# Float32 quarter products for the last 64 queries, one transpose group for the odd blocks, and new planner numbers, in an attention and gated FFN kernel

## The chip, the cores and the metric

The kernel runs on one core of a Trainium2 chip. The metric is the device time of one execution in microseconds. The engines are TensorE (PE in the profile; PEld is its weight load), VectorE (DVE), ScalarE (ACT), GpSimd (POOL) and SyncE (SP), which issues nearly all DMAs. They run side by side and wait for each other through semaphores; each one works in the order in which its instructions were written.

## The reference, cut to what matters

There are 8 batches of 8 heads with 576 queries and 64 columns a head. Attention keeps only scores within `tau` of the row's maximum; the result goes through a gated FFN with a convolution of three taps over the sequence.

```python
scores = scale * np.matmul(q, k.transpose(0, 1, 3, 2))
thresh = np.max(scores, axis=-1, keepdims=True) - tau
scores = np.where(scores >= thresh, scores, -1000000000.0)
scores = scores - np.max(scores, axis=-1, keepdims=True)
attn = np.exp(scores)
attn = attn / (np.sum(attn, axis=-1, keepdims=True) + 1e-09)
x = np.matmul(attn, v)          # then heads side by side: [8, 576, 512]
h = np.maximum(x @ w_in, 0.0)   # w_in [512, 1024]
for k in range(3):
    conv_out += conv_w[k][None, None, :] * hp[:, k:k + S, :]
gate = 1.0 / (1.0 + np.exp(-conv_out))
return (h * gate @ w_out).astype(np.float32)
```

The FFN's weights and the convolution's come as float64.

## The kernel before, in words

**Tiling.** A batch's 576 queries are cut into five tiles, four of 128 and one of 64, and these into two chunks: tiles 0 and 1 (256 queries), tiles 2, 3 and 4 (320). The eight heads go in four pairs. So a batch has 2 chunks x 4 pairs = 8 pair steps, with 2 or 3 units each, 20 units in a batch. A unit is one query tile of one pair of heads. In a full unit each head has its own PSUM tile; in the unit of 64 queries the two heads share one, 64 partitions each.

**A unit** (`unit`, L408 to L490). PE makes the scores into `ps_s` (two tiles). DVE takes the row maximum (`top`, L448), ACT the exponential into `em` (L454), DVE masks it against the limit and sums (`mask`, L457), POOL normalises it (`norm`, L487). `em` is 128 x 1152: two heads of 576 keys, or nine blocks of 128 columns. There are three `em` tiles in rotation.

**The scores' number formats.** In batch 0 (`plain`) they are float32 products with a contraction of 64, and two halves of the keys stand on the two halves of the partitions (L429): for 128 queries two such products lie in the array together, for 64 queries four, in its quarters. From batch 1 on the inputs are split: `prep_k` (L369) scales k by 1/8 on ACT, rounds it to fp32r and has POOL subtract the rest, into `ks`; `prep_q` (L383) rounds q into `q1` and POOL subtracts the rest into `q2`. The scores are then products with a contraction of 128 (L440), one with `q1` and one with `q2` for each head and half of the keys: four for a head, eight for a unit. In the unit of 64 queries the second head is computed with 128 columns of weights and the first then overwrites the upper partitions; its keys are taken turned by 64, for which `ks` holds 64 columns more.

**Turning and attending.** `transposes` (L492) turns `em` on PE (L509) into `ps_t` (two tiles), four blocks a group, and ACT copies each group to `eT` (L503). A full unit has groups of 4, 4 and 1 blocks; the unit of 64 queries has one of 4 and one of two halves (L533). After a pair's last unit, `attend` (L546) multiplies `eT` with v into `pa` (L555, 20 products), and ACT and DVE write x as a rounded part and a rest.

**FFN.** `mm1` (L572) has 12 products for each of 8 blocks of columns into `ph` (L585), then relu, taps, tanh and gate on ACT, POOL and DVE, and the split into the rings `gh` and `gl`. `mm2` (L641) has 24 products into `po` (L650) for each 128 tokens. The FFN work of a chunk is spread over the units of the next chunk.

**Weights.** `split` (L278) turns sixteen float64 pieces of 512 columns into a rounded part and a rest during the first batch: ACT takes the absolute value, POOL limits it from both sides (`f1`, L302), DVE puts the bits together in three steps (L305, L308, L311), ACT rounds (L319) and POOL subtracts (L263). `WRATE` sets how many pieces a unit of the loop gets, for the first and the second matrix.

**Order.** Nothing is issued in the order of the code. Each operation goes to a planner (`Plan`, L53) with an estimated time, the tiles that it reads and writes, and a rank: the number of its unit, less an `AHEAD` value for its sort of work. The planner simulates the five engines and writes the instructions in the order in which it picked them: on each engine the lowest rank that is ready and has its tile free. On PE it may take an operation up to `KEEP` ranks later that needs no costly change of form (`SWITCH`). DVE may take work meant for POOL when more than `BACKLOG` ns of it wait there. The order on each engine is then fixed, and the hardware follows it whatever the real times are.

Of the kernel before, what the change touches and what calls it, by code (L numbers as in the profile page):

```python
# [19 lines left out]
AHEAD = {'s': 4.5, 't': 4.0, 'a': 3.5, 'prep': 5.5, 'w': 2.0, 'load': 4.0}  # L20
# [4 lines left out]
BACKLOG = {'pool': 10000.0, 'dve': 500.0, 'act': 9e9}  # L25
WRATE = (0.9, 0.65)
ALT = 3.0

# [8 lines left out]
KEEP = 0.6  # L37


class Buf:  # L40
# [6 lines left out]
    def __getitem__(self, key):  # L47
        if self.tile is None:
            self.tile = self.pool.tile(self.shape, self.dtype, tag=self.tag, bufs=self.bufs, name=self.name)
        return self.tile[key]  # L50

# [146 lines left out]
def tile_tau_attention_gated_ffn(  # L198
# [26 lines left out]
    GROUPS = [(0, 1), (2, 3, 4)]  # L225
    CHUNKS = [(0, 255), (255, 321)]
    COLS = [(0, 256), (254, 322)]
    NEW = [(0, 256), (256, 320)]
# [49 lines left out]
    def split(src, n, name, high, low, hr, lr, queue="sp"):  # L278
# [3 lines left out]
        stage = plan.buf(wk, "ks", 4, [P, KW], U32, name)  # L282
        value = plan.buf(wk, "q2", 2, [P, 2, QW], U32, f"{name}_f")

        def words(dtype=U32):
            pairs = stage[:, :2 * n].rearrange("p (f two) -> p f two", two=2)
            return pairs[:, :, 0].bitcast(dtype), pairs[:, :, 1].bitcast(dtype)
# [7 lines left out]
        def load():  # L295
            (nc.sync if queue == "sp" else nc.scalar).dma_start(stage[:, :2 * n].bitcast(I64), src)
# [4 lines left out]
        def f1(e):  # L301
            engines[e].tensor_scalar(v(), v(), TINY, HUGE, op0=ALU.max, op1=ALU.min)  # L302
# [23 lines left out]
    KW, QW = 2 * S + D, max(w for _, w in NEW)  # L326
# [30 lines left out]

    def plain(b):
        return b == 0

    def prep_k0(p, g):

        ks = plan.buf(wk, "xk", 2, [P, S + D], F32, f"ks_0_{p}_{g}")
        a = AHEAD["prep"]
        op("sp", 450, lambda: nc.sync.dma_start(ks[:], kp[p]), w=[(ks, 0)], ahead=a + 2)
        op("act", act(S + D), lambda: nc.scalar.activation(ks[:], ks[:], AF.Copy, scale=0.125), w=[(ks, 0)], ahead=a)
        return ks

    def prep_k(b, p, j, ks):  # L369

        w = S + j * D
        a = AHEAD["prep"]
        xk = plan.buf(wk, "xk", 2, [P, S + D], F32, f"xk_{b}_{p}_{j}")
        part = slice(j * S, j * S + w)
        op("sp", 820, lambda: nc.sync.dma_start(xk[:, :w], kd[b, p, :, j, :w]), w=[(xk, 0)], ahead=a + 2)
        op("act", act(w), lambda: nc.scalar.activation(xk[:, :w], xk[:, :w], AF.Copy, scale=0.125), w=[(xk, 0)], ahead=a)
        op("act", act(w), lambda: nc.scalar.activation(ks[:, part], xk[:, :w], AF.Copy), w=[(ks, j)], r=[(xk, 0)], ahead=a)
        op(
            "pool", pool(w), lambda e: subtract(e, ks[D:, part], xk[D:, :w], ks[D:, part].bitcast(F32)),
            w=[(ks, j)], r=[(xk, 0)], ahead=a, other=[("dve", dve(w))]  # L380
        )

    def prep_q(b, p, j, g, q2):  # L383

        o, w = NEW[g]
        n = f"{b}_{p}_{j}_{g}"
        src = qd[b, p, :, j, o:o + w]
        a = AHEAD["prep"]
        if plain(b):
            q1 = plan.buf(wk, "q1", 4, [P, w], F32, f"q1_{n}")  # L390
            op("sp", 455, lambda: nc.sync.dma_start(q1[:], src), w=[(q1, 0)], ahead=a + 2)
            return q1
        xq = plan.buf(wk, "xq", 2, [P, w], F32, f"xq_{n}")
        q1 = plan.buf(wk, "q1", 4, [P, w], F32R, f"q1_{n}")
        op("sp", 455, lambda: nc.sync.dma_start(xq[:], src), w=[(xq, 0)], ahead=a + 2)
        op("act", act(w), lambda: nc.scalar.activation(q1[:], xq[:], AF.Copy), w=[(q1, 0)], r=[(xq, 0)], ahead=a)  # L396
        op(
            "pool", pool(w), lambda e: subtract(e, q2[:, j, :w], xq[:], q1[:].bitcast(F32)),
            w=[(q2, j)], r=[(xq, 0), (q1, 0)], ahead=a, other=[("dve", dve(w))]
        )  # L400
        return q1

    def load_v(b, p, g):
        vt = plan.buf(wk, "v", 2, [P, NBLK + 1, D], F32, f"v_{b}_{p}_{g}")
        op("sp", 820, lambda: nc.sync.dma_start(vt[:], vc[b, p]), w=[(vt, 0)], ahead=AHEAD["prep"])
        return vt

    def unit(u, k, q1, q2, o, n):  # L408
# [5 lines left out]
        em = plan.buf(wk, "em", 3, [P, 2 * S], F32, f"em_{u}")  # L414
# [4 lines left out]
        for h, js in enumerate(heads):  # L419
# [3 lines left out]
            def mm(js=js, ps=ps):  # L423
                if q2 is None:
                    for r, j in enumerate(js):
                        for c in range(2):
# [3 lines left out]
                                ps[r * n:(r + 1) * n, c, :CH], lhsT=q1[j][on, o:o + n], rhs=k[on, at:at + CH],  # L430
# [3 lines left out]


                for r, j in reversed(list(enumerate(js))):
                    for c in range(2):
                        at = j * S + r * D + c * CH
                        for i, q in enumerate((q1[j][:, o - r * n:o + n], q2[:, j, o - r * n:o + n])):
                            nc.tensor.matmul(  # L440
                                ps[:(r + 1) * n, c, :CH], lhsT=q, rhs=k[:, at:at + CH], start=(i == 0), stop=(i == 1)
                            )
# [13 lines left out]
            def mask(ps=ps, th=th, view=view, total=total):  # L456
# [6 lines left out]
                "pe", 480 if q2 is None else 532 * len(js), mm, w=[(ps, 0)],  # L463
                r=[(x, j if x is not k or q2 is not None else 0) for j in js for x in (k, q2) if x is not None] + [(q1[j], 0) for j in js],
                ahead=a, kind="rows" if q2 is None else "full"
# [26 lines left out]
    def transposes(u, em, n, eT, off):  # L492
        def group(i, js, parts, *evacs):
# [4 lines left out]
                "pe", max(width, 140) * 0.86, lambda: parts(pt), w=[(pt, 0)], r=[(em, j) for j in js] + [(ident, 0)], ahead=AHEAD["t"],  # L498
                kind="turn"
# [7 lines left out]
        def turn(pt, b0, nb):  # L507
            for i in range(nb):
                nc.tensor.transpose(  # L509
                    out=pt[:, i * P:(i + 1) * P], in_=em[:, (b0 + i) * P:(b0 + i + 1) * P], identity=ident[:]  # L510
                )

        if n == P:
            for b0 in range(0, NBLK, 4):
                nb = min(4, NBLK - b0)
                js = [j for j in range(2) if b0 * P < (j + 1) * S and (b0 + nb) * P > j * S]
                group(
                    b0, js, lambda pt, b0=b0, nb=nb: turn(pt, b0, nb),
                    (nb * P, lambda b0=b0, nb=nb: eT[:, b0:b0 + nb, off:off + P],
                     lambda pt, nb=nb: pt[:, :nb * P].rearrange("p (a b) -> p a b", a=nb))  # L520
                )
            return
# [8 lines left out]
        def halves(pt):  # L531
            for j in range(2):
                nc.tensor.matmul(  # L533
                    pt[j * D:(j + 1) * D, :n], lhsT=em[:, 4 * P:4 * P + D], rhs=ident[:, j * n:(j + 1) * n], start=True, stop=True
                )

        group(
            0, [0], lambda pt: turn(pt, 0, 4),
            (4 * P, both, lambda pt: pt[:].rearrange("p (i j n) -> p j i n", i=4, j=2))
        )  # L540
        group(
            1, [0], halves,
            (n, lambda: eT[:, 4, off:off + n], lambda pt: pt[:, :n])
        )
# [27 lines left out]
    def mm1(b, g, f, xs):  # L572
        gh, gl = ring
        k0, kn = CHUNKS[g]
        a0, an = COLS[g]
        fs = slice(f * P, (f + 1) * P)
        n = f"{b}_{g}_{f}"
# [4 lines left out]
        for cb in range(NCB):  # L582
# [8 lines left out]
            op("pe", an * 3 / 2.4 + 40, mm, w=[(ph, 0)], r=ws + [(xs[cb], i) for i in (0, 1, 2) if i < 2 or g], kind="full")  # L591
# [70 lines left out]
    def ffn(c):  # L662

        first = []
        if c < len(chunks):
            b, g = chunks[c]
            first = [(COLS[g][1] * 5, lambda f=f: mm1(b, g, f, xs[c])) for f in range(NFB)]
        ends = [0, EARLY] + [(b * S + sum(CHUNKS[g])) // P for b, g in chunks]
        second = [(5120, lambda m=m: mm2(m)) for m in range(ends[c], ends[c + 1])]
        seq = []  # L670
        n1, n2 = MOE
        if not c:
# [6 lines left out]
    CW = COLS[1][1]  # L679
    xs = {}  # L680
    chunks = [(b, g) for b in range(B) for g in range(2)]
    pairs = [(c, p) for c in range(len(chunks)) for p in range(NP)]
    units = [(i, t) for i in range(len(pairs)) for t in GROUPS[pairs[i][0] % 2]]
    kss, qss, q2s, vts = {}, {}, {}, {}

    def prep(i, j):
# [15 lines left out]
        if j == 0:
            vts[i] = load_v(b, p, g)
# [98 lines left out]
```

## Time and profile before

| | |
|---|---|
| median of 3 runs | 1002.08 us (999.22 to 1002.26) |
| profiled execution | 1003.37 us, span 1001.6 us, mean granted clock 0.977 |
| PE busy | 947.2 us (95%) |
| DVE busy | 802.7 us (80%) |
| POOL busy | 757.7 us (76%) |
| ACT busy | 705.0 us (70%) |
| DMA | 79.00 MB, mean 79 GB/s |

A group's row gives line, engine, operation, what is written and read, shapes and count; then busy time and mean ns of one; then the idle time of the engine before them and who ended it. Matmuls overlap, so that the mean of one is longer than its share. In a timeline a row starts with its start and its duration. A row of a stretch gives, after its bounds and length, the busy time and count of PE, PEld, DVE, ACT and POOL, then the granted clock, the DMA share and GB/s.

### The profile page before, as it was taken

How to read it: one execution, taken by the hardware profiler on the slowest of the kernel's cores; microseconds unless marked ns; L12 is line 12 of the kernel's file. 1: busy time of each engine (PE TensorE's matmuls, PEld its weight loads, DVE VectorE, ACT ScalarE, POOL GpSimd, SP SyncE). 2: the span in 40 equal slices, each digit the busy share in tenths (PEclk: the TensorE clock that was granted, in tenths of full speed). 3: DMA queues.
4: the chain of work that ended last, by engine and by line, in shares of the span. 5: the costliest groups of instructions: out<-in, count | busy, mean ns of one | idle time of the engine just before them, and what ended most of it. 6: DMA issues, size and time to landing. Idle time of an engine off the chain costs nothing.

```text
span 1001.6 us, 19333 instructions
## 1 busy us (share of the span) xinstructions
PE 947.2 (95%) x6368; PEld 766.5 (77%) x6368; DVE 802.7 (80%) x1942; ACT 705.0 (70%) x1544; POOL 757.7 (76%) x1159
## 2 busy tenths in 40 slices
PE   5788868999999999999999999999999999999998
PEld 2445636877888788877888788878888878888796
DVE  4879969998777967998888978898788888898443
ACT  4666668787776776778767777778776777776443
POOL 3878998887877887798677877788767877787343
PEclk9889969999999999999999999999999999999999
DMA  6543224133222232223321233213321231211000
GB/s 197 156 124 122 81 72 124 53 87 98 75 79 60 83 93 65 64 68 90 97 64 58 78 92 91 65 41 106 99 67 58 66 106 46 64 54 38 22 22 32
DMA packets 44739, 79.00 MB, mean 79 GB/s; under 512 B 5216, under 2 KB 21600, under 8 KB 44640
## 3 DMA queue, kind: packets, MB, share of 16 engines
q1 hardware_dynamic: 44208, 76.20, 25.0%
q10 hardware_dynamic: 432, 1.57, 0.5%
q8 instruction: 51, 0.84, 0.3%
q14 instruction: 48, 0.39, 0.1%
HBM read 68.31 MB, written 9.44 MB: 78 GB/s over the span
## 4 chain that ended last, share of the span: by engine, by line
PE 69%; POOL 14%; DVE 9%; issue 4%; ACT 4%; DMA 1%; SPq 0%; POOLq 0%; ACTq 0%
PE po L650 16%; PE ph L585 15%; PE pa L555 13%; PE ps_s L440 12%; PE ps_t L509 12%; POOL em L487 5%; DVE em L457 2%; POOL gl L263 2%; POOL ks L263 2%; DVE few L448 2%; POOL stage_f L302 1%; DVE t L612 1%; POOL q L263 1%; ACT eT L503 1%; PE ps_s L429 1%
## 5 line engine op out<-in xcount | busy, mean ns | idle before, releaser
L487 POOL TENSOR_SCALAR em<-em,few 128x576 f32<-128x576 f32 x288 | 260.5, 912 | 40.3 <-DVE few L482 29.0
L448 DVE TENSOR_REDUCE few<-ps_s 128x1 f32<-128x576 f32 x288 | 212.9, 750 | 66.9 <-PE ps_s L440 51.4
L457 DVE SCALAR_TENSOR_TENSOR em<-ps_s,few,em 128x576 f32<-128x576 f32 x288 | 232.0, 811 | 33.6 <-ACT em L454 28.0
L585 PE MATMUL ph<-x,w1h 128*128 128x322 f32 (+1 forms) x1024 | 254.1, 310 | 1.0 <-DVE x L566 0.8
L503 ACT ACTIVATE eT<-ps_t 128x512 f32<-128x512 f32 (+1 forms) x448 | 200.4, 480 | 63.9 <-PE ps_t L509 60.6
L454 ACT ACTIVATE em<-ps_s,few 128x576 f32<-128x576 f32 x288 | 211.8, 743 | 44.0 <-DVE few L448 33.4
L509 PE MATMUL ps_t<-ident,em 128*128 128x128 f32 x1280 | 206.0, 283 | 20.2 <-POOL em L487 14.6
L509 PEld LDWEIGHTS ps_t<-ident,em 128*128 128x128 f32 x1280 | 154.1, 144 | 63.4 <-POOL em L487 32.9
L440 PE MATMUL ps_s<-ks,q 128*128 128x288 f32 (+1 forms) x1120 | 193.8, 305 | 6.7 <-DVE em L457 6.6
L612 DVE SCALAR_TENSOR_TENSOR t<-hp,cw,t 128x255 f32<-128x255 f32 (+1 forms) x256 | 171.1, 675 | 23.0 <-POOL t L603 19.6
L585 PEld LDWEIGHTS ph<-x,w1h 128*128 128x128 f32 x1024 | 178.8, 190 | 8.2 <-issue 3.6
L555 PE MATMUL pa<-eT,v 128*64 128x256 f32 (+1 forms) x1280 | 174.8, 421 | 1.7 <-ACT eT L503 1.7
L440 PEld LDWEIGHTS ps_s<-ks,q 128*128 128x128 f32 (+1 forms) x1120 | 159.7, 184 | 20.9 <-issue 10.1
L585 PE MATMUL ph<-x,w1l 128*128 128x322 f32 (+1 forms) x512 | 152.1, 297 | 0.0
L555 PEld LDWEIGHTS pa<-eT,v 128*64 128x64 f32 x1280 | 88.2, 140 | 70.2 <-issue 10.2
L263 POOL TENSOR_TENSOR gl<-t,gh 128x321 fp32r<-128x321 f32 (+13 forms) x184 | 118.9, 658 | 23.5 <-ACT gh L629 22.3
L650 PE MATMUL po<-w2h,gh 128*128 128x512 f32 x288 | 121.1, 421 | 0.8 <-ACT w2h L319 0.8
L650 PE MATMUL po<-w2l,gh 128*128 128x512 f32 x288 | 113.9, 396 | 2.0 <-POOL w2l L263 2.0
L650 PE MATMUL po<-w2h,gl 128*128 128x512 f32 x288 | 113.9, 396 | 1.2 <-POOL gl L263 0.8
L263 POOL TENSOR_TENSOR q<-xq,q 128x256 fp32r<-128x256 f32 (+1 forms) x112 | 94.0, 846 | 14.6 <-ACT q L396 8.3
L603 POOL TENSOR_SCALAR t<-hp,cw 128x321 f32<-128x321 f32 (+1 forms) x128 | 72.3, 566 | 43.1 <-ACT hp L600 37.5
L585 PEld LDWEIGHTS ph<-x,w1l 128*128 128x128 f32 x512 | 97.6, 191 | 0.5
(56 smaller groups left out, 1122.8 us busy)
## 6 DMA issues: line engine op xcount, KB each, us to landing
v<-in_vc_dram SPq DMA_DIRECT2D x64, 320.0 KB, 2.9
out_dram<-ot SPq DMA_DIRECT2D x36, 256.0 KB, 2.1
xk<-in_kd_dram SPq DMA_DIRECT2D x28, 320.0 KB, 2.9
xq<-in_qd_dram SPq DMA_DIRECT2D x56, 160.0 KB, 2.2
xk<-in_kd_dram SPq DMA_DIRECT2D x28, 288.0 KB, 2.7
xq<-in_qd_dram SPq DMA_DIRECT2D x56, 128.0 KB, 2.1
stage<-in_w_out_dram SPq DMA_DIRECT2D x8, 512.0 KB, 3.3
ks<-in_kp_dram SPq DMA_DIRECT2D x8, 320.0 KB, 3.8
```

Source lines behind the costliest of these rows:

```text
L263: engines[e].tensor_tensor(dst, x, y, op=ALU.subtract)
L440: nc.tensor.matmul(ps[:(r + 1) * n, c, :CH], lhsT=q, rhs=k[:, at:at + CH], start=(i == 0), stop=(i == 1))
L448: nc.vector.tensor_reduce(few[:rows, nm], ps[:rows, :, :CH], op=ALU.max, axis=mybir.AxisListType.XY, negate=True)
L454: nc.scalar.activation(view(), ps[:rows, :, :CH], AF.Exp, bias=few[:rows, nm])
L457: nc.vector.scalar_tensor_tensor(view(), ps[:rows, :, :CH], few[:rows, th], view(), op0=ALU.is_ge, op1=ALU.mult, accum_out=few[:rows, total])
L487: engines[e].tensor_scalar(sl, sl, few[:rows, 6 + h:7 + h], few[:rows, 8 + h:9 + h], op0=ALU.mult, op1=ALU.add)
L503: "act", act(w, True), lambda dst=dst, src=src: nc.scalar.activation(dst(), src(pt), AF.Copy),
L509: nc.tensor.transpose(out=pt[:, i * P:(i + 1) * P], in_=em[:, (b0 + i) * P:(b0 + i + 1) * P], identity=ident[:])
L555: nc.tensor.matmul(pa[j * D:(j + 1) * D, :w], lhsT=vt[:, blk + j, :], rhs=eT[:, blk, :w], start=(r == 0), stop=(r == 4))
L585: nc.tensor.matmul(ph[:, :an], lhsT=w1[w][:, cb, fs], rhs=xs[cb][:, h, :an], start=(cb == 0 and i == 0), stop=(cb == NCB - 1 and i == 2))
L612: nc.vector.scalar_tensor_tensor(t[:, :kn], hp[:, k:kn + k], cw[:, 3 * f + k:3 * f + k + 1], t[:, :kn], op0=ALU.mult, op1=ALU.add)
L650: nc.tensor.matmul(po[:], lhsT=x[:, f, at:at + P], rhs=w[:, f, :], start=(f == 0 and i == 0), stop=(f == NFB - 1 and i == 2))
```

## The change

- The last unit of a pair (64 queries) has float32 products in quarters of the array in all batches, as in batch 0. For that, `prep_rows` loads k as two halves on the partitions into an `xk` tile and the unit's q into a new tile `q`, and scales q by 1/8 (batch 0 now scales q too, not k). `ks` loses its 64 extra columns, and the split of q covers the 256 queries of full units alone. `q1` is one tile for both heads.
- The ninth block of a pair's full units, and the halves of its unit of 64 queries, are turned in one group after the pair's last unit. `em` has four tiles.
- `f1` takes the smaller of value and upper limit first, and then the larger of that and the lower limit.
- The planner's numbers are others: `AHEAD`, `BACKLOG`, `WRATE`, `KEEP`.
- The chunks are written as a list of named tuples; their cuts and the tokens of each stay the same.

```diff
-AHEAD = {'s': 4.5, 't': 4.0, 'a': 3.5, 'prep': 5.5, 'w': 2.0, 'load': 4.0}
+AHEAD = {'s': 6.0, 't': 3.5, 'a': 3.5, 'prep': 4.0, 'w': 2.0, 'load': 4.25}
-BACKLOG = {'pool': 10000.0, 'dve': 500.0, 'act': 9e9}
-WRATE = (0.9, 0.65)
+BACKLOG = {'pool': 28000.0, 'dve': 500.0, 'act': 9000000000.0}
+WRATE = (0.891, 1.015)
-KEEP = 0.6
+KEEP = 1.2
...
         def f1(e):
-            engines[e].tensor_scalar(v(), v(), TINY, HUGE, op0=ALU.max, op1=ALU.min)
+            engines[e].tensor_scalar(v(), v(), HUGE, TINY, op0=ALU.min, op1=ALU.max)
...
+    def prep_rows(i, b, p, o, w, tag):
+
+        k = plan.buf(wk, "xk", 2, [P, S + D], F32, f"k_{i}")
+        q = plan.buf(wk, tag, 2, [P, 2, w], F32, f"{tag}_{i}")
         a = AHEAD["prep"]
+        op("sp", 450, lambda: nc.sync.dma_start(k[:], kp[b, p]), w=[(k, 0)], ahead=a + 2)
+        op("sp", 450, lambda: nc.sync.dma_start(q[:], qd[b, p, :, :, o:o + w]), w=[(q, 0)], ahead=a + 2)
+        op("act", act(2 * w), lambda: nc.scalar.activation(q[:], q[:], AF.Copy, scale=0.125), w=[(q, 0)], ahead=a)
+        return k, q
...
-        em = plan.buf(wk, "em", 3, [P, 2 * S], F32, f"em_{u}")
+        em = plan.buf(wk, "em", 4, [P, 2 * S], F32, f"em_{u}")
...
                             nc.tensor.matmul(
-                                ps[r * n:(r + 1) * n, c, :CH], lhsT=q1[j][on, o:o + n], rhs=k[on, at:at + CH],
+                                ps[r * n:(r + 1) * n, c, :CH], lhsT=q1[on, j, o:o + n], rhs=k[on, at:at + CH],
                                 start=True, stop=True
                             )
                     return
-
-
-                for r, j in reversed(list(enumerate(js))):
-                    for c in range(2):
-                        at = j * S + r * D + c * CH
-                        for i, q in enumerate((q1[j][:, o - r * n:o + n], q2[:, j, o - r * n:o + n])):
-                            nc.tensor.matmul(
-                                ps[:(r + 1) * n, c, :CH], lhsT=q, rhs=k[:, at:at + CH], start=(i == 0), stop=(i == 1)
-                            )
+                for c in range(2):
+                    for i, q in enumerate((q1, q2)):
+                        nc.tensor.matmul(
+                            ps[:, c, :CH], lhsT=q[:, h, o:o + n], rhs=k[:, h, c * CH:(c + 1) * CH], start=(i == 0), stop=(i == 1)
+                        )
...
+        if len(ems) < tiles:
+            return
+        full = [x for x in ems if x[1] == P]
+        w = len(full) * P
+
+        def odd(pt):
+            for i, x in enumerate(full):
+                turn(pt, i * P, x[0], 8)
+            if n < P:
+                halves(pt, w)
+
+        parts = [(w, lambda: eT[:, 8, :w], lambda pt: pt[:, :w])]
+        if n < P:
+            parts.append((n, lambda: eT[:, 4, off:off + n], lambda pt: pt[:, w:w + n]))
+        group(8, [(x[0], 1) for x in full] + ([(em, 0)] if n < P else []), odd, *parts)
...
+            if not o:
+                prep_k(b, p, j, whole[i][0])
+            prep_q(i, b, p, j, *whole[i][1:])
+            if j and w % P:
+                last[i] = (*prep_rows(i, b, p, o + w - w % P, w % P, "q"), None)
```

More of the change, by code (lines that the diff above doesn't have):

```diff
@@ L1 @@
+import collections
 import heapq
@@ L50, in __getitem__ @@
         return self.tile[key]
+Chunk = collections.namedtuple("Chunk", "b tiles new cols tokens done")
 class Plan:
@@ L222, in tile_tau_attention_gated_ffn @@
     TILES = [(t * P, min(P, S - t * P)) for t in range((S + P - 1) // P)]
[L225 to L228, printed above, removed]
+    chunks = []
+    for b in range(B):
+        for tiles in FIRST if not b else GROUPS:
+            o = TILES[tiles[0]][0]
+            end = sum(TILES[tiles[-1]])
+            a0, k0 = max(o - 2, 0), max(o - 1, 0)
+            chunks.append(Chunk(
+                b=b, tiles=tiles, new=(o, end - o), cols=(a0, end - a0), tokens=(k0, (end if end == S else end - 1) - k0),
+                done=(b * S + (end if end == S else end - 1)) // P
+            ))
+    XW = [max(c.cols[1] for c in chunks[i::2]) for i in range(2)]
+    CW = max(XW)
     cpool = ctx.enter_context(tc.tile_pool(name="cpool", bufs=1))
@@ L325, in tile_tau_attention_gated_ffn @@
     WN = 512
-    KW, QW = 2 * S + D, max(w for _, w in NEW)
+    QW = 2 * P
     n3 = 3 * NFB
@@ L490, in unit, with transposes, group @@
         return em
-    def transposes(u, em, n, eT, off):
-        def group(i, js, parts, *evacs):
+    def transposes(u, ems, tiles, eT):
+        em, n, off = ems[-1]
+        def group(i, reads, parts, *evacs):
             pt = plan.buf(ps_t, "ps_t", 2, [P, 512], F32, f"ps_t_{u}_{i}")
@@ L497, in group @@
             op(
[L498 to L499 removed]
+                "pe", max(width, 140) * 0.86, lambda: parts(pt), w=[(pt, 0)], r=reads + [(ident, 0)], ahead=AHEAD["t"], kind="turn"
             )
@@ L505, in group, with turn, turns @@
                 )
[L507 to L522, printed above, removed]
+        def turn(pt, at, em, b):
+            nc.tensor.transpose(out=pt[:, at:at + P], in_=em[:, b * P:(b + 1) * P], identity=ident[:])
+        def turns(pt, b0):
+            for i in range(4):
+                turn(pt, i * P, em, b0 + i)
         def both():
@@ L665, in ffn @@
         if c < len(chunks):
[L666 to L669, printed above, removed]
+            first = [(chunks[c].cols[1] * 5, lambda f=f: mm1(c, f, xs[c])) for f in range(NFB)]
+        done = [chunks[i].done if i >= 0 else 0 for i in (c - 2 + (c - 1 < EARLY), c - 1 + (c < EARLY))]
+        second = [(5120, lambda m=m: mm2(m)) for m in range(*done)]
         seq = []
         n1, n2 = MOE
-        if not c:
+        if c < EARLY:
             return first + second
@@ L677, in ffn @@
         return seq
-    CW = COLS[1][1]
     xs = {}
-    chunks = [(b, g) for b in range(B) for g in range(2)]
     pairs = [(c, p) for c in range(len(chunks)) for p in range(NP)]
-    units = [(i, t) for i in range(len(pairs)) for t in GROUPS[pairs[i][0] % 2]]
-    kss, qss, q2s, vts = {}, {}, {}, {}
+    units = [(i, t) for i in range(len(pairs)) for t in chunks[pairs[i][0]].tiles]
+    whole, last, vts = {}, {}, {}
     def prep(i, j):
@@ L735, in tile_tau_attention_gated_ffn @@
                 attend(i, eT, vts[i], w, x, off)
-            if t == GROUPS[g][0]:
-                prep(i + 1, 0)
-            if t == GROUPS[g][1]:
-                prep(i + 1, 1)
-            if t == GROUPS[g][-1] and p == NP - 1:
+            for j in range(2):
+                if t == tiles[min(j, len(tiles) - 1)]:
+                    prep(i + 1, j)
+            if t == tiles[-1] and p == NP - 1:
                 seq = ffn(c)
@@ L744, in tile_tau_attention_gated_ffn @@
                 for ns, fn in seq:
-                    work.append((now + 1 + at / total * NP * len(GROUPS[1 - g]), fn))
+                    work.append((now + 1 + at / total * NP * len(chunks[min(c + 1, len(chunks) - 1)].tiles), fn))
                     at += ns
```

140 lines of the change are left out of this document (62 added, 78 removed).

## The prediction

> **What bounds the kernel now.** I read the page's busy shares first, then the busy time by stretch, then the chain of waits of the start.
>
> ```profile
> PE 947.2 (95%) x6368; PEld 766.5 (77%) x6368; DVE 802.7 (80%) x1942; ACT 705.0 (70%) x1544; POOL 757.7 (76%) x1159
> ```
>
> TensorE leads, but a mean over stages hides that there are two regimes:
>
> ```profile
> 0.00:25.00 25.00, 12.54 (x54) 6.90 (x56) 11.98 (x34) 11.67 (x21) 9.18 (x23) 1.00 0.61 197
> 25.00:125.00 100.00, 83.02 (x513) 52.98 (x510) 87.73 (x201) 64.64 (x130) 84.88 (x95) 0.88 0.38 121
> 125.00:175.00 50.00, 37.06 (x202) 26.14 (x201) 39.85 (x86) 35.30 (x71) 43.18 (x45) 0.80 0.33 98
> 200.00:900.00 700.00, 692.56 (x4835) 578.41 (x4834) 584.06 (x1444) 525.65 (x1170) 550.55 (x867) 1.00 0.25 76
> 900.00:1001.60 101.60, 97.38 (x596) 80.74 (x594) 55.19 (x124) 48.15 (x113) 48.85 (x98) 0.99 0.08 28
> ```
>
> The columns are busy PE, weight loads, DVE, ACT and POOL, then the granted clock. From 200 to 900 us PE is busy 692.56 of 700 at clock 1.00, while DVE, ACT and POOL have 16 to 25% of their time free. There the end moves only with PE's own instructions, or with its 7.4 us of idle time. Before 175 us it is otherwise: PE idles 12.5 + 17.0 + 12.9 = 42.4 us, and its clock falls to 0.88 and 0.80, while DVE and POOL are 80 to 88% busy. In that time the sixteen weight pieces are split and PE has little FFN work to fill it.
>
> ```profile
> by line: issue 9.7%; POOL em L487 9.6%; PE pa L555 8.2%; PE ps_t L509 7.0%; POOL stage_f L302 6.7%; DVE em L457 5.6%; PE ps_s L429 4.9%; DVE few L448 4.2%; DMA ks<-in_kp_dram 3.0%; POOL ks L263 2.9%; ACT eT L503 2.8%; DVE stage_f L308 2.6%;
> L302 POOL TENSOR_SCALAR stage_f<-stage_f x16: 1915/1942/2335, 13.0 to 144.3; 128x512 f32<-128x512 f32 x16
> ```
>
> This is the chain of the first 200 us. The two limits of the weights (L302) hold 6.7% of it, 13.4 us; each takes 1.94 us.
>
> **The quarters.** In batches 1 to 7 the unit with the last 64 queries is eight single-pass (fp32r) products of 288 columns. In batch 0 it is already four float32 products in quarters of the array, which the trace records as eight. Both forms can thus be timed, from the first start to the start of the next group:
>
> ```profile
> 311.62 1.22 PE L440 MATMUL ps_s<-ks,q 128*128 128x288 f32 x8
> 312.67 0.31 PE L585 MATMUL ph<-x,w1h 128*128 128x322 f32 x1
> ```
> ```profile
> 88.16 0.28 PE L585 MATMUL ph<-x,w1h 128*128 128x256 f32 x1
> 88.37 0.71 PE L429 MATMUL ps_s<-ks,q 64*64 64x288 f32 x8
> 89.02 0.39 PE L585 MATMUL ph<-x,w1h 128*128 128x256 f32 x1
> 89.24 0.28 PE L585 MATMUL ph<-x,w1l 128*128 128x256 f32 x1
> 89.36 0.28 PE L585 MATMUL ph<-x,w1h 128*128 128x256 f32 x1
> ```
>
> Now: 312.67 − 311.62 = 1.05 us. In quarters: 89.02 − 88.37 = 0.65 us, and the change of form costs on both sides. The `ph` product ahead of it waits 0.21 us for its successor and the one behind it 0.22, where the interval 89.24 to 89.36 is 0.12; so 0.09 + 0.10 are added and a unit costs 0.84. The gain is 0.21 us. There are 28 such units (7 batches, 4 pairs), all in the stretch that PE bounds: **−5.9 us**. Bounds: with the crossings free, 28 × (1.05 − 0.65) = 11.2; with crossings that eat all of it, 0. I take the measured crossing, as the neighbours in batch 1 to 7 are the same `ph` and transposes.
>
> [...]
>
> **The odd blocks in one group.** The ninth 128-column block of each full unit had a transpose, a PSUM tile and an evacuation of its own. Now the odd blocks of a pair's units share one group. On PE that is no gain, since a lone transpose costs hardly more than itself:
>
> ```profile
> 304.57 0.32 PE L585 MATMUL ph<-x,w1h 128*128 128x322 f32 x1
> 304.73 0.27 PE L509 MATMUL ps_t<-ident,em 128*128 128x128 f32 x1
> 304.76 0.39 PE L585 MATMUL ph<-x,w1h 128*128 128x322 f32 x1
> 304.99 0.31 PE L585 MATMUL ph<-x,w1l 128*128 128x322 f32 x1
> 305.14 0.31 PE L585 MATMUL ph<-x,w1h 128*128 128x322 f32 x1
> ```
>
> From 304.57 to 304.99 are 0.42 us with two `ph` products of 0.15 (304.99 to 305.14) in it: 0.12 us for the transpose. In a group of eight each further one takes (1.03 − 0.27)/7 = 0.11:
>
> ```profile
> 302.51 1.03 PE L509 MATMUL ps_t<-ident,em 128*128 128x128 f32 x8
> ```
>
> So joining the odd blocks of 64 pairs saves at most some 64 × 2 × 0.01 = 1.3 us on PE; I take 0. ACT loses two evacuations of 128 columns a pair and gains one of 256:
>
> ```profile
> L503 ACT ACTIVATE eT<-ps_t 128x128 f32<-128x128 f32 x128 | 35.6, 278 | 6.9 <-PE ps_t L509 6.4
> L503 ACT ACTIVATE eT<-ps_t 128x512 f32<-128x512 f32 x288 | 169.7, 598 | 57.0 <-PE ps_t L509 54.2 <-ACT xk L376 0.2
> ```
>
> Between these rows a column costs 0.83 ns, so 256 take about 385 ns: 35.6 − 64 × 0.385 = 11 us less of ACT's 705. ACT is idle a quarter of the long stretch, so this moves nothing; if ACT were the bound it would be worth the 11 us. What the edit may cost is the life of `em` (fourth rival).
>
> **Splitting and loading for the last units.** POOL's second subtraction per pair shrinks from 640 to 576 columns, and the q split of the second chunk from 320 to 256:
>
> ```profile
> L263 POOL TENSOR_TENSOR ks<-xk,ks 64x640 fp32r<-64x640 f32 x28 | 46.2, 1652 | 1.7
> L263 POOL TENSOR_TENSOR ks<-xk,ks 64x576 fp32r<-64x576 f32 x28 | 41.0, 1463 | 2.2
> L263 POOL TENSOR_TENSOR q<-xq,q 128x320 fp32r<-128x320 f32 x56 | 51.3, 923 | 8.6 <-ACT q L396 4.2 <-ACT eT L503 2.2 <-ACT x L563 1.6
> L263 POOL TENSOR_TENSOR q<-xq,q 128x256 fp32r<-128x256 f32 x56 | 42.7, 770 | 6.0 <-ACT q L396 4.1 <-ACT xk L376 1.4 <-ACT eT L503 0.2
> ```
>
> That is 28 × 0.19 + 56 × 0.15 = 14 us less on POOL, off the path after 200 us (POOL 550 of 700 busy) and 1.4 us of it before 175. ACT saves about as many columns on the same edits as its 28 new scalings of 128 columns of q (0.28 us each by the 128-column row) add: nothing. SP issues 28 more loads of k (320 KB) and 28 of q (64 KB). They sit in SP's queue ahead of the next pair's q and v loads, and the k tile holds one of the two `xk` buffers until the quarters have read it. A load of that size takes 2.9 us to land here, and a unit of the loop lasts (938.3 − 148.3)/140 = 5.6 us by the next row (1120 products, eight a unit); that covers it: 0. Without that cover it is 28 × 2.9 = 81 us at the worst, which I do not believe, as the DMA share is 0.25.
>
> ```profile
> L440 PE MATMUL ps_s<-ks,q x1120: 288/295/580, 148.5 to 938.4; 128*128 128x288 f32 x167, 128*64 128x288 f32 x20
> xk<-in_kd_dram SPq DMA_DIRECT2D x28, 320.0 KB, 2.9
> ```
>
> **The order of limits.** The same two immediates on POOL, min first and then max. The trace has no min-first row. Nearest rows: 1.94 us for max-first, and 0.83 us, the median of a multiply-add over 576 columns:
>
> ```profile
> L487 POOL TENSOR_SCALAR em<-em,few x288: 811/829/1810, 15.2 to 943.2; 128x576 f32<-128x576 f32 x144
> ```
> It is thus worth 0 to 16 × 1.1 = 18 us of POOL, all before 146 us. I take 0: same operations, same count. [...]
>
> **Planner numbers.** The pieces of the second weight matrix come at ranks 1/1.015 apart, not 1/0.65: the eighth at 9.0 + 7.9 = 16.9 units, not 21.2. Today the first output product runs while these pieces arrive:
>
> ```profile
> 126.52 0.50 PE L650 MATMUL po<-w2h,gh 128*128 128x512 f32 x1 [0.77 <-ACT w2h L319]
> ...
> 128.62 0.50 PE L650 MATMUL po<-w2l,gh 128*128 128x512 f32 x1 [1.37 <-POOL w2l L263]
> ...
> 137.48 1.12 PE L509 MATMUL ps_t<-ident,em 128*128 128x128 f32 x4 [2.33 <-ACT w2h L319]
> ...
> 140.83 0.80 PE L650 MATMUL po<-w2l,gh 128*128 128x512 f32 x1 [0.67 <-POOL w2l L263]
> 141.56 5.60 PE L555 MATMUL pa<-eT,v 128*64 128x320 f32 x20
> ```
>
> Direct waits on w2: 0.77 + 1.37 + 2.33 + 0.67 = 5.1 us. After them the `pa` group of 20 takes 5.60 us, at the lowered clock; by the next row a group takes 97.5/32 = 3.05 (640 products, 20 each): 2.6 more. Up to 7.7 us can go.
>
> ```profile
> L555 PE MATMUL pa<-eT,v 128*64 128x320 f32 x640 | 97.5, 453 | 1.7 <-ACT eT L503 1.7
> ```
> But the pieces move into 75 to 125 us, where DVE and POOL are 88 and 85% full, and there the limits alone cost POOL 1.94 us a piece and delay a softmax. Lower bound −7.7, upper +5 (two pieces' POOL and DVE time that finds no gap). I take **−4**. The other ranks, the larger backlog before DVE takes POOL's work, and PE's wider choice (KEEP 1.2) only reorder work; in the dense stretch they can win no more than the 7.4 us of idle time and I take 0.
>
> **Sum.** The profiled execution took 1003.37 us, 1.8 beyond its span; −5.9 − 4.0 gives 993.5. The runs' median lies 1.3 below the profiled time: **992.2 us**.
>
> **The rivals.**
> 1. *Min-first is cheap on POOL.* For it: a multiply-add over more columns takes 0.83 us on the same engine. Against: symmetry. It frees 18 us of POOL before 146 us. L302's 13.4 us in the chain is the most that can return; DVE, 88% busy there, keeps some back, so I take 10. Time 982, 974 to 990.
> 2. *Nothing arrives.* PE's 0.21 us a unit turns into idle time because the score tiles wait for DVE's mask, and the earlier w2 gives back at the start what it took. For it: PE's waits for `em L457` exist already. Against: 5.9 us of PE work less, with 116 us of free DVE time in the long stretch. Time 1000.5, 999 to 1004.
> 3. *The softmax tile becomes the bound, slower.* A pair of three units now holds three of four `em` tiles until its last unit is normalised on POOL, because the odd group comes then; only one tile is left for the next pair, where three rotated freely before. Behind the odd group in PE's order stand the pair's `pa` products, which read what it evacuates.
>
> ```profile
> PE ps_t L509 <- POOL em L487: 14.6, 18, 3.7
> ```
>
> Each such wait of PE costs 14.6/18 = 0.8 us today. If 16 of the 32 three-unit pairs add one, that is 13 us, and net of the quarters +7: 1009 us, 1005 to 1020. It decides from eight pairs on (8 × 0.8 > 5.9). Against: PE has FFN work to run instead, and the order is planned with that tile count.
>
> **How the numbers follow.** This kernel's three runs span 0.3%, so 0.3% (3 us) is what a measurement can tell from no change. Chances: forecast 0.44 (992, own range 985 to 1000), rival 1 0.28, rival 2 0.14, rival 3 0.14. Faster than 999.1: 0.40 of the forecast's 0.44, all of rival 1, 0.01 of rival 2: 0.69. Within 0.3%: 0.04 of the forecast and 0.11 of rival 2. Slower: 0.02 of rival 2 and rival 3: 0.16. The range runs from rival 1's lower edge to the near half of rival 3: 974 to 1007.
>
> **What would show it.** Right: the 64-query group from its first start to the next group is 0.65 us in all batches, with 0.2 us intervals on both sides; PE busy in 200 to 900 stays above 98.5%; the last w2 wait of PE ends before 135 us. The new L302 row settles rival 1: under 1.2 us it holds, at 1.9 it is out. Rival 3 shows as PE waits on `em L487` above 30 us in all. The forecast is wrong if the start (PE idle before 175 us, 42.4 now) grows, or if the quarters among fp32r products show more than 0.9 us.

## The result and the profile after

The changed kernel takes **978.31 us** (977.8 to 978.69, 4 runs) against 1001.87 us before (999.22 to 1002.26): a ratio of 0.977, 95% interval 0.9753 to 0.9788. The profiled execution took 977.8 us with a span of 976.0, that is 25.6 us less than before. The forecast was 992 us: right in sign, and less than half of the gain. The result lies below the 985 to 1000 us that the forecast gave itself; it is inside the whole range only because rival 1's 974 to 990 us was added to it.

The busy time of the changed kernel by stretch (columns as before):

```profile
0.00:25.00 25.00, 9.07 (x33) 5.06 (x33) 11.24 (x25) 11.32 (x21) 9.46 (x27) 1.00 0.66 219
25.00:125.00 100.00, 82.27 (x540) 51.46 (x540) 90.44 (x210) 69.00 (x133) 79.81 (x107) 0.93 0.39 123
125.00:175.00 50.00, 43.41 (x293) 34.89 (x293) 46.47 (x111) 39.89 (x82) 45.34 (x57) 0.93 0.32 95
...
200.00:900.00 700.00, 694.16 (x4911) 569.31 (x4911) 598.17 (x1459) 526.15 (x1163) 546.00 (x894) 1.00 0.29 88
900.00:976.00 76.00, 71.91 (x421) 60.04 (x419) 33.56 (x70) 30.71 (x75) 27.73 (x56) 1.00 0.07 25
```

The first 175 us in one row, before and then after:

```profile
0.00:175.00 175.00, 132.63 (x764) 86.02 (x765) 139.56 (x319) 111.61 (x221) 137.24 (x161) 0.87 0.40 125
0.00:175.00 175.00, 134.75 (x864) 91.41 (x865) 148.15 (x343) 120.20 (x234) 134.62 (x189) 0.94 0.41 129
```

PE's busy time hardly moved: by 2.1 us up to 175 us and by 1.6 us between 200 and 900. What moved is how much PE had done by then. Up to 175 us it had issued 864 products, before it was 764; between 200 and 900 us it is 4911 instead of 4835, with 5.8 us of idle time instead of 7.4. So busy time is the wrong count, and for the comparison I priced each product with its usual distance to the next start, in us: 0.132 for scores of 288 columns, 0.108 a transpose, 0.149 and 0.119 for `ph` with 322 and 256 columns, 0.228 for `po`, 0.142 and 0.116 for `pa`, 0.172 and 0.105 for float32 scores in halves and in quarters, 0.075 for the odd halves. The 0.105 is the forecast's own 0.84 us over eight, crossings included, so the work column repeats the forecast's term and does not measure it. Priced so, PE's work is 889.0 us before and 882.9 after; the rest of the span is lost to waits, crossings and the slow clock:

```
                 work    lost to 175   175 to 900   after 900    span
before           889.0       74.2         31.4         7.0      1001.6
after            882.9       62.1         25.3         5.7       976.0
difference        -6.1      -12.1         -6.1        -1.3       -25.6
```

The forecast had the first column and a third of the second. The granted clock rose too, from 0.87 to 0.94 in the first 175 us, and how much of the 12.1 us is the clock's isn't separated. In the changed kernel's four executions, the mean clock was 0.990 once and 0.984 three times, and their times lie within 0.9 us of each other. The limits of the weights, by line, and the chain of the first 200 us after the change, where they no longer appear among the leading lines:

```profile
L322 POOL TENSOR_SCALAR stage_f<-stage_f x16: 612/614/1174, 9.7 to 122.3; 128x512 f32<-128x512 f32 x16
by line: PE pa L571 8.7%; DMA q<-in_qd_dram 8.6%; issue 8.2%; POOL em L495 8.2%; PE ps_s L442 7.6%; PE ps_t L519 6.2%; DVE em L466 5.8%; PE ps_s L449 4.9%; PE ph L600 4.5%; DVE few L457 4.4%; PE po L665 3.5%; DVE stage_f L331 2.4%; DVE stag
```

A limit takes 0.61 us instead of 1.94: 16 × 1.33 = 21 us of POOL are gone. The chain also has 8.6%, 17 us, on loads of q: 8.4 of them ahead of the first product, the rest at 39 and 49 us.

### The profile page after: what moved, and what is told of

It reads as the page before. It is cut to its first block, busy times and chain, and to the rows that moved or that the text cites. A ratio compares the mean times of both kernels' runs of the same rounds, so it can differ in the third digit from the quotient of the medians.

```text
span 976.0 us, 19384 instructions
## 1 busy us (share of the span) xinstructions
PE 925.7 (95%) x6368; PEld 740.6 (76%) x6368; DVE 804.6 (82%) x1926; ACT 694.8 (71%) x1508; POOL 728.6 (75%) x1175
## 4 chain that ended last, share of the span: by engine, by line
PE 74%; DVE 10%; POOL 7%; issue 3%; DMA 2%; ACT 2%; SPq 0%; POOLq 0%; DVEq 0%; ACTq 0%
PE ph L600 17%; PE po L665 17%; PE pa L571 13%; PE ps_t L519 12%; PE ps_s L449 11%; PE ps_s L442 3%; DVE em L466 3%; POOL em L495 3%; DMA q<-in_qd_dram 2%; DVE few L457 2%; POOL gl L280 2%; DVE t L627 1%; DVE t L634 1%; POOL t L618 1%; PE ps_t L534 1%
## 5 line engine op out<-in xcount | busy, mean ns | idle before, releaser
L495 POOL TENSOR_SCALAR em<-em,few 128x576 f32<-128x576 f32 x288 | 263.5, 922 | 42.4 <-DVE few L490 29.3
L463 ACT ACTIVATE em<-ps_s,few 128x576 f32<-128x576 f32 x288 | 209.0, 740 | 42.0 <-DVE few L457 31.5
L514 ACT ACTIVATE eT<-ps_t 128x512 f32<-128x512 f32 (+2 forms) x384 | 193.8, 532 | 48.0 <-PE ps_t L519 44.8
L519 PE MATMUL ps_t<-ident,em 128*128 128x128 f32 x1280 | 191.5, 279 | 12.0 <-POOL em L495 8.1
L627 DVE SCALAR_TENSOR_TENSOR t<-hp,cw,t 128x255 f32<-128x255 f32 (+1 forms) x256 | 176.6, 693 | 29.8 <-POOL t L618 28.1
L519 PEld LDWEIGHTS ps_t<-ident,em 128*128 128x128 f32 x1280 | 148.9, 142 | 52.3 <-POOL em L495 17.4
L571 PE MATMUL pa<-eT,v 128*64 128x256 f32 (+1 forms) x1280 | 171.5, 415 | 0.0
L449 PE MATMUL ps_s<-ks,q 128*128 128x288 f32 x896 | 159.4, 306 | 7.8 <-DVE em L466 3.2
L449 PEld LDWEIGHTS ps_s<-ks,q 128*128 128x128 f32 x896 | 131.2, 189 | 23.3 <-issue 7.4
L280 POOL TENSOR_TENSOR ks<-xk,ks 64x576 fp32r<-64x576 f32 x56 | 81.7, 1460 | 16.5 <-ACT ks L398 10.2
```

The costliest lines, as they stand in the source:

```text
L280: engines[e].tensor_tensor(dst, x, y, op=ALU.subtract)
L449: nc.tensor.matmul(ps[:, c, :CH], lhsT=q[:, h, o:o + n], rhs=k[:, h, c * CH:(c + 1) * CH], start=(i == 0), stop=(i == 1))
L463: nc.scalar.activation(view(), ps[:rows, :, :CH], AF.Exp, bias=few[:rows, nm])
L495: engines[e].tensor_scalar(sl, sl, few[:rows, 6 + h:7 + h], few[:rows, 8 + h:9 + h], op0=ALU.mult, op1=ALU.add)
L514: "act", act(w, True), lambda dst=dst, src=src: nc.scalar.activation(dst(), src(pt), AF.Copy),
L519: nc.tensor.transpose(out=pt[:, at:at + P], in_=em[:, b * P:(b + 1) * P], identity=ident[:])
```

## The experiments

All times are medians; the kernel before was run beside each set (1000.8 to 1002.3 us). The times that follow are compared with 978.3 us for the changed kernel and 1001.9 for the one before. The changed kernel was not run again beside the sets; as the kernel before differs by 1.6 us between them, differences of 2 us or less say nothing.

**e1 and e2: the order of limits alone.** In the changed kernel it is put back, in the kernel before it is put in.

```diff
-            engines[e].tensor_scalar(v(), v(), HUGE, TINY, op0=ALU.min, op1=ALU.max)
+            engines[e].tensor_scalar(v(), v(), TINY, HUGE, op0=ALU.max, op1=ALU.min)
```

> The changed kernel with the limits on GpSimd back in the old order (max, then min); nothing else, so the planner writes the same order of instructions. Theory A (the cheap order is the missing term: 16 limits of 1.94 instead of 0.61 us, 21 us of GpSimd given back to the first 130 us): 8 to 16 us slower than the changed kernel, 986 to 994 us, all of it before 200 us. Theory B (the planner's new numbers made the start shorter and the limits were hidden): at most 4 us slower, below 983 us.

> The kernel before with only the order of the limits changed to min, then max. Theory A: 9 to 16 us faster than before, 986 to 993 us, with TensorE idle before 175 us falling from 42.4 to about 30 us. Theory B: less than 4 us faster, above 998 us.

e1 takes 987.6 us (ratio to before 0.9859, 0.9838 to 0.9881), e2 993.7 us (0.9916, 0.9895 to 0.9938). So the order is worth 9.2 us in the one and about 8 us in the other, at the lower edge of theory A and clear of theory B. e2 is just outside the 9 to 16 us that theory A gave for it, and PE's idle time before 175 us falls from 42.4 to 36.5 us and not to 30. The limits of e1 and its first 175 us, then the same of e2:

```profile
L322 POOL TENSOR_SCALAR stage_f<-stage_f x16: 1913/1938/2492, 9.1 to 133.4; 128x512 f32<-128x512 f32 x16
0.00:175.00 175.00, 130.10 (x778) 87.06 (x780) 138.21 (x317) 111.82 (x214) 141.68 (x173) 0.89 0.39 123
```
```profile
L302 POOL TENSOR_SCALAR stage_f<-stage_f x16: 610/614/1036, 12.6 to 137.9; 128x512 f32<-128x512 f32 x16
0.00:175.00 175.00, 138.50 (x830) 90.45 (x831) 142.85 (x338) 117.99 (x235) 125.46 (x174) 0.88 0.41 128
```

The price follows the order, to a hundredth of a microsecond. What is lost by 175 us is 72.7 in e1 (62.1 in the changed kernel) and 65.8 in e2 (74.2 in the kernel before); after 175 us both lose what their parents lose. The clock doesn't explain it: in e2 it is 0.88, before 0.87, and 8.4 us of loss are gone all the same. Of 21 us of POOL, 8 to 9 reach the end. DVE probably takes its share back, 142.85 us busy of 175 in e2 and 148.15 in the changed kernel, where it was 139.56; no run tests that.

**e11: max-first, with its true price told to the planner.**

```diff
...   # the order of e1, and:
-        op("pool", n * 1.69 + 80, f1, w=[a], ahead=w, other=[("dve", 150 + n * 0.65)])
+        op("pool", n * 3.32 + 243, f1, w=[a], ahead=w, other=[("dve", 150 + n * 0.65)])
```

> Max-first limits in the changed kernel (987.6 us), with the planner told their measured price, 1.94 us for 512 columns, where it reckons with 0.95. If the loss of 9 us comes from an order written for a cheaper limit, most of it comes back: 979 to 983 us. If it is GpSimd's time itself that binds the start, 985 to 990 us.

987.5 us (0.9855, 0.9829 to 0.9881), as e1. So the loss is POOL's time, not an order written for a cheaper limit. The profiled execution was the fastest of the four, 984.5 us, at a clock of 0.94 in the start (0.89 in e1): it loses 65.5 us by 175 us and 2.9 us more than e1 up to 900. Where the loss falls is thus less certain than its size.

**e3, e7, e10, e13: the planner's numbers.** e3 has all four old ones in the changed kernel; e7, e10 and e13 change the scores' lead alone, to 4.5, 5.5 and 6.5.

```diff
-AHEAD = {'s': 6.0, 't': 3.5, 'a': 3.5, 'prep': 4.0, 'w': 2.0, 'load': 4.25}
+AHEAD = {'s': 4.5, 't': 3.5, 'a': 3.5, 'prep': 4.0, 'w': 2.0, 'load': 4.25}   # e7
```

> The changed kernel with the planner's four old numbers (ranks ahead, backlog, rate of weight pieces, width of choice). Theory A: within 5 us of the changed kernel, 974 to 984 us. Theory B: 10 us or more slower, above 988 us.

> The changed kernel with one old number, the rank of the scores (4.5 ahead instead of 6.0). With all four old numbers it was at 1005 us, 27 us slower, with 19 us of that lost after 175 us. If the scores' lead is what the four em tiles and the shared group need, 10 us or more slower here, 988 us or more, with TensorE waiting for the masked and normalised em. If it is another number, or only the sum of all, less than 4 us slower.

> The changed kernel with the scores 5.5 ahead: between 6.0 (978.3 us) and 4.5 (995.9 us). If the lead acts by degrees, 982 to 986 us. If each schedule is a draw of its own that any small edit turns, anywhere between 972 and 998 us, and then terms of a few microseconds can't be read off single edits in this kernel.

> The changed kernel with the scores 6.5 ahead. So far 4.5 gave 995.9, 5.5 gave 985.9 and 6.0 gave 978.3 us. If the lead acts by degrees, 970 to 978 us. If 6.0 is a lucky or a tuned point, above 981 us.

e3 takes 1005.0 us (ratio to before 1.0025, 1.0007 to 1.0043): with the old numbers the whole change brings nothing, the cheap limits included. Beside e2, which has the same limits and numbers, the new structure even costs 1005.0 − 993.7 = 11.3 us. Theory A's side claim, that the numbers matter little, fell here. The lead gives 995.9 us at 4.5, 985.9 at 5.5, 978.3 at 6.0 and 979.5 at 6.5: by degrees up to 6.0 and flat beyond, which neither expectation of e13 had. Where e3 and e7 lose most of it, between 200 and 900 us:

```profile
200.00:900.00 700.00, 684.68 (x4779) 553.96 (x4778) 561.61 (x1401) 516.11 (x1131) 539.91 (x881) 1.00 0.29 86
```
```profile
200.00:900.00 700.00, 690.09 (x4826) 557.76 (x4827) 580.08 (x1434) 519.65 (x1146) 538.33 (x876) 1.00 0.30 86
```

PE idles 15.3 us in e3 and 9.9 in e7, where the changed kernel idles 5.8, and issues 4779 and 4826 products there instead of 4911. The 9.1 us between e7 and e3 belong to the other numbers together; no run parts them. The wait for the normalised `em` is back in e3 (19.0 us in 26 waits, 8.1 us in 12 in the changed kernel):

```profile
PE ps_t L519 <- POOL em L495: 19.0, 26, 2.5
```
```profile
PE ps_t L519 <- POOL em L495: 8.1, 12, 1.3
```

From 175 to 900 us alone it is, in e3, e7 and the changed kernel:

```profile
PE ps_t L519 <- POOL em L495: 5.9, 13, 1.6
PE ps_t L519 <- POOL em L495: 3.8, 9, 1.1
PE ps_t L519 <- POOL em L495: 0.2, 1, 0.2
```

**e6: the new numbers and min-first limits in the kernel before.**

```diff
-AHEAD = {'s': 4.5, 't': 4.0, 'a': 3.5, 'prep': 5.5, 'w': 2.0, 'load': 4.0}
+AHEAD = {'s': 6.0, 't': 3.5, 'a': 3.5, 'prep': 4.0, 'w': 2.0, 'load': 4.25}
-BACKLOG = {'pool': 10000.0, 'dve': 500.0, 'act': 9e9}
-WRATE = (0.9, 0.65)
+BACKLOG = {'pool': 28000.0, 'dve': 500.0, 'act': 9e9}
+WRATE = (0.891, 1.015)
-KEEP = 0.6
+KEEP = 1.2
...   # and the order of limits, as in e2
```

> The kernel before with min-first limits and the planner's four new numbers; its scores, its groups and its three em tiles stay. If the new numbers are good by themselves (second weight matrix earlier, scores further ahead), it is 5 to 12 us faster than the kernel before with min-first limits alone (993.7 us): 982 to 989 us. If they only fit the structure they were chosen for, it is within 4 us of 993.7 us, or slower.

994.8 us (0.9935, 0.9909 to 0.996), beside 993.7 of e2: the numbers do nothing for the old structure. With them and the same limits, the new structure is worth 994.8 − 978.3 = 16.5 us. Lost by 175 us are 63.4 us, in e2 65.8; the 2.4 us won at the start are given back later.

**e4, e14, e15: the quarters.** e4 takes the eight fp32r products back (with the 64 more columns of `ks` and the wider q split); e14 does that and sets the scores' lead to 4.5; e15 leaves the quarters in and gives POOL 56 more subtractions, whose results are the values that stand there already.

```diff
...
-                for c in range(2):
-                    for i, q in enumerate((q1, q2)):
-                        nc.tensor.matmul(
-                            ps[:, c, :CH], lhsT=q[:, h, o:o + n], rhs=k[:, h, c * CH:(c + 1) * CH], start=(i == 0), stop=(i == 1)
-                        )
+                for r, j in reversed(list(enumerate(js))):
+                    for c in range(2):
+                        at = j * S + r * D + c * CH
+                        for i, q in enumerate((q1[:, j, o - r * n:o + n], q2[:, j, o - r * n:o + n])):
+                            nc.tensor.matmul(
+                                ps[:(r + 1) * n, c, :CH], lhsT=q, rhs=k[:, at:at + CH], start=(i == 0), stop=(i == 1)
+                            )
...
```

> The changed kernel with the unit of 64 queries in batches 1 to 7 as eight fp32r products again (with its 64 extra columns of k and its share of the q split). By the prediction's term (28 units of 1.05 instead of 0.84 us): 6 us slower, 983 to 986 us. Theory C (the quarters carry the part that the prediction missed, through score tiles that come free sooner and 14 us less of GpSimd): 12 us or more slower, above 990 us. If it is within 2 us, the term was not there.

> The changed kernel without the quarters (993.1 us alone) and with the scores 4.5 ahead (995.9 us alone). If the two act by themselves, the losses add: 1008 to 1014 us. If each pays only together with the other, no more is lost than by one of them: 992 to 999 us.

> The changed kernel with one more subtraction of 64 columns on GpSimd after each q split of the second chunk, which writes the same values again: 56 of about 0.35 us, 20 us of GpSimd in all, more than the 14 us that the quarters save there. If the quarters' worth beyond their 6 us is GpSimd's relief, 6 us or more slower, 984 us or more. If GpSimd is covered by TensorE, within 3 us of 978 us.

e4 takes 993.1 us (0.9912, 0.9896 to 0.9928): 14.8 us slower, theory C's side. By the prices its work is 889.0 us, 6.1 more; that is the prediction's own term, taken over and not measured here. Another 7.8 us are lost between 175 and 900 us (33.1 instead of 25.3). e14 takes 998.7 us (0.9959, 0.9943 to 0.9975). By themselves the two would have made 978.3 + 14.8 + 17.6 = 1010.7. So with the scores 6.0 ahead the quarters are worth 14.8 us, with 4.5 ahead 998.7 − 995.9 = 2.8; and without quarters the lead is worth 5.7 us instead of 17.6. Most of what each brings needs the other.

e15 takes 983.9 us (0.9811, 0.9786 to 0.9837): 5.6 us slower for

```profile
L280 POOL TENSOR_TENSOR q<-xq,q 128x64 fp32r<-128x64 f32 x56 | 22.5, 401 | 1.0
200.00:900.00 700.00, 690.87 (x4879) 564.12 (x4873) 593.88 (x1449) 520.50 (x1152) 558.69 (x937) 1.00 0.29 87
```

22.5 us of POOL. That is near the bound of 6 that I set, and neither expectation holds cleanly: POOL, 78% busy in this stretch, isn't fully covered by PE, since its operations stand in the order that PE waits for (9.1 us of PE idle). By that rate the 14 us that the quarters spare POOL are worth some 14 × 5.6/22.5 = 3.5 us, an estimate, of the 7.8. It may be too high, as the added operation also writes `q2`, which the scores read, and can delay them directly.

**e5, e9: the shared group of odd blocks, and the fourth `em` tile.** e5 turns the odd blocks one by one again; e9 does that with three `em` tiles.

```diff
-        if len(ems) < tiles:
-            return
...
-        group(8, [(x[0], 1) for x in full] + ([(em, 0)] if n < P else []), odd, *parts)
+            group(8, [(em, 0)], lambda pt: halves(pt, 0), (n, lambda: eT[:, 4, off:off + n], lambda pt: pt[:, :n]))
+        else:
+            group(8, [(em, 1)], lambda pt: turn(pt, 0, em, 8), (P, lambda: eT[:, 8, off:off + P], lambda pt: pt[:, :P]))
```

> The changed kernel with the odd blocks turned one by one again (a group, a tile of PSUM and an evacuation for each full unit, as before); four em tiles, quarters, min-first and the new numbers stay. By the prediction's term (at most 1.3 us of TensorE, 11 us of ScalarE that is off the path): within 3 us of the changed kernel, 976 to 982 us. If the shared group is what makes the dense stretch better (fewer PSUM tiles and evacuations between products), 984 us or more, lost in 200 to 900 us. If holding em long is a cost (the slower rival of the prediction), it is faster than the changed kernel, below 975 us.

> The changed kernel with lone odd groups (975.4 us) and three em tiles instead of four; with lone groups an em tile is free as soon as its own unit is turned. If the fourth tile is what lets the scores run 6.0 ahead, 8 us or more slower, 983 us or more, with TensorE idle before em in the dense stretch. If the lead works without it, within 4 us of 975 us.

e5 takes 975.4 us (972.0 to 975.7; 0.9738, 0.9714 to 0.9761) and e9 973.7 (971.2 to 976.7; 0.9721, 0.9694 to 0.9747). That is between the first and the last expectation of e5. The shared group brings nothing and seems to cost some 3 us, at the edge of what the intervals tell apart; once it is gone, the fourth `em` tile is not needed either. So the gain at the lead of 6.0 needs neither of them. Whether the loss at 4.5 comes from the longer life of `em`, no run with lone odd groups at 4.5 tells; in e7 all nine waits on `em` from 175 to 900 us stand ahead of ordinary groups of four transposes, none ahead of a shared group.

**e8, e12: the first loads.** e8 puts the first k and q ahead of the weights on SP's queue (`load` 3.9 instead of 4.25); e12 does that with lone odd groups.

> The changed kernel with the loads of the weights at rank 3.9 ahead instead of 4.25, so that the first k and q are issued on SyncE's queue before the convolution's and the first weights. In the changed kernel the first product starts at 11.2 us, before it was 5.8 us. If those 5 us are on the path, 3 to 5 us faster, 973 to 975 us. If the start is set by VectorE's and GpSimd's sum of work up to 150 us, within 2 us of 978 us.

> Both edits that were not slower than the changed kernel: lone odd groups, and the first k and q ahead of the weights. If they add up, 974 us (975.4 less 1.4); if the schedule is a draw, 971 to 985 us.

The change had a cost that the prediction didn't see. First score product before, then in the changed kernel:

```profile
5.79 2.29 PE L429 MATMUL ps_s<-ks,q 64*128 64x288 f32 x8 [5.79 <-ACT ks L366]
```
```profile
11.16 2.29 PE L442 MATMUL ps_s<-k,q 64*128 64x288 f32 x8 [11.16 <-ACT q L389]
```

PE starts 5.4 us later. e8 takes 976.9 us (0.9763, 0.9744 to 0.9781), 1.4 us less, within the intervals of the changed kernel: the late start is all but hidden. That fits DVE and POOL setting the pace up to 150 us, the second expectation, but no run shows the reason. e12 takes **973.2 us** (972.2 to 974.2; 0.9713, 0.9692 to 0.9734), as if the two added up. It is faster than both kernels; it does not overlap the changed kernel's interval.

## Why the prediction was right or wrong

**The quarters, −5.9: the unit's price is right, its worth in place is not.** The same group in the dense stretch of the changed kernel:

```profile
342.30 0.28 PE L600 MATMUL ph<-x,w1h 128*128 128x256 f32 x1
342.51 0.72 PE L442 MATMUL ps_s<-k,q 64*64 64x288 f32 x8
343.15 0.39 PE L600 MATMUL ph<-x,w1h 128*128 128x256 f32 x1
343.38 0.28 PE L600 MATMUL ph<-x,w1l 128*128 128x256 f32 x1
```

0.64 us from its start to the next, 0.21 and 0.23 around it where 0.12 is usual: 0.84, as forecast from batch 0. The change of form costs 0.09 and 0.11 us here, where batch 0 showed 0.09 and 0.10. The planner often puts the group behind the `pa` products, whose last step is as long without it: from the start of the last `pa` product of 320 columns it is 0.36 us to a group of quarters and 0.36 to a transpose, where 0.26 is usual from one pair of `pa` products to the next:

```profile
213.15 1.78 PE L571 MATMUL pa<-eT,v 128*64 128x320 f32 x12
214.86 0.72 PE L442 MATMUL ps_s<-k,q 64*64 64x288 f32 x8
215.51 0.66 PE L519 MATMUL ps_t<-ident,em 128*128 128x128 f32 x4
```

Eleven of the 26 units between 200 and 900 us follow `pa` so, which spares an estimated 11 × 0.09 = 1 us. But undone, the quarters cost 14.8 us and not 5.9 (2.8 with the lead at 4.5). The 7.8 us that e4 loses between 175 and 900 us beyond its work had no term in the sum.

**The order of limits, taken as 0: wrong, and the largest single miss.** The failing step is "I take 0: same operations, same count". Min-first costs 0.61 us, a third of max-first, below the multiply-add that served as the nearest row. With the limits put back (e1) the rest of the change is worth 1001.9 − 987.6 = 14.3 us where the sum had 9.9; so of the 13.9 us between forecast and result, 9.2 are this step. Rival 1 was right in mechanism and in its term (10 us taken, 8 to 9 measured), though the 18 us of POOL that bounded it were 21. Its 982 us lies 4 us above the result because the rest brought more than the sum had. I gave it 0.28 by symmetry, which the trace could not show. The price per column follows from the rows of 24 columns, before and after, beside those of 512:

```profile
L302 POOL TENSOR_SCALAR stage_c_f<-stage_c_f x1: 323/323/323, 9.9 to 9.9; 128x24 f32<-128x24 f32 x1
L322 POOL TENSOR_SCALAR stage_c_f<-stage_c_f x1: 206/206/206, 9.2 to 9.2; 128x24 f32<-128x24 f32 x1
```

Min-first is (614 − 206)/488 = 0.84 ns a column, where max-first is (1942 − 323)/488 = 3.3. That the price is the same in either order was my inference, which no run had shown. The measurement decides.

**The planner numbers, −4 at the start and 0 later: not settled at the start, wrong later.** PE's waits on w2 (5.1 us before) are gone; the last waits of its kind in that place are for others:

```profile
131.00 0.66 PE L449 MATMUL ps_s<-ks,q 128*128 128x288 f32 x3 [2.64 <-POOL q L280]
...
133.48 0.80 PE L665 MATMUL po<-w2h,gl 128*128 128x512 f32 x1 [1.59 <-POOL gl L280]
```

By all that is not the limits, the start gained 74.2 − 72.7 = 1.5 us with max-first (before to e1) and 65.8 − 62.1 = 3.7 with min-first (e2 to the changed kernel). By the numbers alone it gained 2.4 in the old structure (e2 to e6) and 8.1 in the new one (70.2 in e3). So 4 is among what the runs show, but no single value is. The second step that failed is this one: "in the dense stretch they can win no more than the 7.4 us of idle time and I take 0". It failed twice. The bound was wrong, since a product's record runs on past the usual start of the next one, and a wait shorter than this tail shows as busy. The tail is about 0.16 us here, an estimate from the prediction's rows: a lone transpose is shown 0.27 us long, and in a group the next one starts 0.11 us after it. A longer wait is shown short by as much: in the changed kernel a `ph` product shown 0.28 us long starts at 204.82 us and the next product at 205.81, 0.87 us later than the usual 0.12, and 0.70 of it show as idle time. From the changed kernel to e7, 11.8 us more are lost between 175 and 900 us, and only 4.7 us of it show as idle time. And 0 was wrong: the lead of the scores alone is worth 17.6 us to the new structure. In the changed kernel this stretch lost 6.1 us less.

**The odd blocks, 0: right within 3 us.** The `em` rival's sign may be right too (e5 is 3 us faster), far below its price; PE's waits on `em` fell from 14.6 to 8.1 us instead of rising. ACT's evacuation of 256 columns takes 386 ns, 385 forecast:

```profile
L514 ACT ACTIVATE eT<-ps_t 128x256 f32<-128x256 f32 x64 | 24.7, 386 | 7.3 <-PE ps_t L519 6.1 <-PE ps_t L534 0.7
```

**Splitting and loading, 0: right for SP**, whose 56 more loads show nowhere in PE's waits; not quite for POOL's 14 us (e15). The loads of q that now stand in the chain of the start belong to batch 0, of which the prediction said nothing; e8 tests the first of them alone.

**What stays open:** why quarters and lead pay only together. The loss without either doesn't show as one wait of PE. From 175 to 900 us the changed kernel waits 0.2 us on the normalised `em`, 0.4 on `gl` and 2.1 on DVE's mask before the scores; without quarters (e4) it is 2.6, 3.8 and 3.1 us, with the lead at 4.5 (e7) 3.8, 2.5 and 1.3, and many more are too short to show. The order that the planner writes differs from kernel to kernel, so no single edit tells it apart. The signs that the prediction set for being right all came (0.64 us a group, PE 99.2% busy in the dense stretch, no PE wait on w2, 40.3 us of idle time before 175 us), so they could not tell 992 from 978 us; only the row of the limits could.

## What to carry to other kernels

Where the trace doesn't show a form, a range from "nothing" to "all" with the point taken at "nothing" is a guess: if the operation stands in the chain (13 us of the first 200 here), its price in the new form decides the forecast, and the likeliest case should be split there. In a kernel whose order is written by a planner, a structural edit and the planner's numbers must be costed together: with the limits equal, the same structure cost 11 us with the old numbers and gained 16.5 with the new ones. And PE's busy time is no measure of its slack when waits shorter than a product's recorded tail (about 0.16 us here) count as busy; count the products done in a stretch.

## What the runs showed of the hardware that was not expected

GpSimd's two-step limit of 512 float32 columns takes 0.61 us as min then max and 1.94 us as max then min, in eight kernels (614 ns in the changed kernel, e2 and e6, 613 in e5 and e7; 1942 before, 1938 in e1, 1940 in e11). A transpose, an evacuation and a PSUM tile of its own for a lone 128-column block cost PE nothing that these runs can show (e5 takes 975.4 us, the changed kernel 978.3).
